# Far chunks of a chunked scan before a tanh network: log rows broadcast by DMA, y and state in one product, C B^T of two chunks at a time; the first chunks' state in its own bank

## The chip, the core and the metric

The kernel runs on one core of one Trainium2 chip. The metric is the device time of one execution in microseconds; the median of several runs is given. The core has five engines that run side by side: TensorE (PE), VectorE (DVE), ScalarE (ACT), GpSimd (POOL), and SyncE (SP), which here issues every DMA.

## The reference

Inputs: `x` (4, 8, 768, 32), decays `a` (4, 8, 768), `B` and `C` (4, 8, 768, 16), all float32; weights `w_in` (256, 2048) and `w_out` (2048, 256), float64.

```python
for c in range(nc):                       # chunks of 32 steps in the reference
    la = log_a[:, :, sl]
    cum = np.cumsum(la, axis=-1)
    L = np.exp(cum[:, :, :, None] - cum[:, :, None, :]) * causal
    M = np.einsum('bhin,bhjn->bhij', Cc, Bc) * L
    y_intra = np.einsum('bhij,bhjd->bhid', M, xc)
    y_inter = np.einsum('bhin,bhnd->bhid', Cc, state) * np.exp(cum)[:, :, :, None]
    y[:, :, sl] = y_intra + y_inter
    Bx = np.einsum('bhjn,bhjd->bhjnd', Bc, xc) * np.exp(cum[:, :, -1:] - cum)[:, :, :, None, None]
    state = np.exp(np.sum(la, axis=-1))[:, :, None, None] * state + np.sum(Bx, axis=2)
...
x = y.transpose(0, 2, 1, 3).reshape(3072, 256)
h = x @ w_in
g = h - np.tanh(h)
out = (g @ w_out).astype(np.float32)
```

## The kernel before

**The scan.** The result does not depend on the chunk length, so the kernel cuts each batch of 768 steps into seven chunks of 112 (`Q`), the last of 96; there are 28 chunks, 0 to 27. On the 128 partitions of a chunk's tiles the first 16 (`N`) hold the incoming state and the other 112 the steps, so state and steps go through the same products. For each chunk:

- `att`: PE makes C B^T of the eight heads (`bc` holds both; 32 rows a product, four products side by side). In `bc` POOL puts the 16x16 identity (`idn`) in the state's rows.
- `lt`: the decays between steps. For chunks 0 to 2 (`first_tile`) PE sums the logs into `cp` in a `ph` bank, and ACT takes the exponential with `ncum` as bias, one instruction for each head. For all later chunks (`chunk_a`) the log differences come as PE products in bfloat16 from three-part splits of the running sums: `lt_c` (ones and parts) times `rt_c` (parts and signs) into the first half of the `att` tile, and ACT takes one exponential over all heads. The parts go out to DRAM once (`cum3`, `put_parts`) and come back in small loads (`get_parts`), in two slices `SPAN`.
- DVE multiplies `att` into `lt`, POOL cuts it to the causal part (`affine_select`).
- `chunk_y`: PE multiplies `x` with `lt` into `y` (eight products of 112 columns), and `x` with the decayed `B` (`bw`, made by POOL in `prep`) into the next state in the same bank (eight products of 32 columns). ACT copies the state into the first 16 rows of the next chunk's `x` (four copies) and rounds `y` into `xh`; DVE makes the remainder `xl`.

**The network** runs transposed on token tiles (`WIDTH`: four of 256, four of 512). Each factor is a rounded part and a remainder (`wh`, `wl`, `xh`, `xl`, `gh`, `gl`), and three of the four part products are taken. `mm1` is the first product into a `ph` bank (two exist), `act` the tanh (ACT), the subtraction (DVE), rounding (ACT) and remainder (DVE), and `mm2` the second product into `po0`/`po1`. The weights arrive as float64 bits in `raw` and are turned into `wh` and `wl` by ACT and DVE (`conv`). The first four tiles run in sweeps over four blocks of the middle dimension (`SWEEPS`), so that work can begin while weights come in; the other four run over all 16 at once.

**Order.** All work goes through `Order`: each piece names its engine, a cost, what it reads and writes; a list planner (`search`) with these costs and priorities then fixes the order in which each engine's queue gets its instructions. Each engine runs its queue in order. Chunks from `JOINT` (10) on are called far here; in them C B^T of a chunk is issued together with y of the chunk before it as one PE step, and y takes a `ph` bank instead of `po1`.

## Time and profile before

| | |
|---|---|
| median of 3 runs | 338.89 us (338.74 to 338.98) |
| the profiled execution | 338.04 us, its span 336.3 us |
| busy: PE, DVE, ACT, POOL | 323.7, 227.8, 193.5, 51.4 us |
| DMA | 22.85 MB |

Columns of the profile's lines: in a timeline the start and the duration in us, the engine, the line of the kernel, the operation, what it writes and reads, and in brackets the idle time ahead with what ended it. A PE row's duration reaches past the start of the next row because products are pipelined, so steps of PE are measured from start to start. An f32 product shows as two records (x8 for four products). In a table of stretches: the stretch, its length, then for PE, PE's weight loads, DVE, ACT and POOL the busy time and instructions, then the granted PE clock (1.00 is full speed), the DMA share and GB/s. In a list of waits: who waited for whom, us in total, times, longest.

### The profile page before, as it was taken

What the parts mean: (1) busy time and instruction counts of PE and PEld (TensorE: products, weight loads), DVE (VectorE), ACT (ScalarE), POOL (GpSimd) and SP (SyncE); (2) the same over time, 40 slices, a digit from 0 to 9 for tenths busy, and PEclk for the clock granted to TensorE, in tenths of its full rate; (3) what the DMA queues carried; (4) which work ended last, traced back from release to release, by engine and by line L of the source; (5) the groups of instructions that cost most, each with busy time, mean ns of one, the idle gap of its engine ahead of it and who ended that gap; (6) DMA issues with size and microseconds to landing.
All of it is one profiled execution on the core that took longest, in us unless ns stands there. A gap on an engine that the chain in (4) does not pass through costs nothing.

```text
span 336.3 us, 6854 instructions
## 1 busy us (share of the span) xinstructions
PE 323.7 (96%) x2764; PEld 273.5 (81%) x2764; DVE 227.8 (68%) x335; ACT 193.5 (58%) x399; POOL 51.4 (15%) x69
## 2 busy tenths in 40 slices
PE   8666999999999999999999999999999999999995
PEld 7545889999999999877787777877787787888884
DVE  5979989999899866565655575555565554644452
ACT  8857589677476434555565564555455553544441
POOL 1546442120300111011112012111011010000000
PEclk9957799999999999999999999999999999999999
DMA  6567835441000015302111110300010000100001
GB/s 197 185 207 261 248 127 188 141 125 59 2 1 2 2 33 178 119 7 71 44 48 43 32 56 34 107 2 1 2 62 3 0 2 0 62 2 0 0 2 62
DMA packets 12111, 22.85 MB, mean 68 GB/s; under 512 B 2672, under 2 KB 5400, under 8 KB 12080
## 3 DMA queue, kind: packets, MB, share of 16 engines
q1 hardware_dynamic: 12080, 22.42, 20.7%
q8 instruction: 22, 0.36, 0.5%
q14 instruction: 9, 0.07, 0.1%
HBM read 19.10 MB, written 3.32 MB: 67 GB/s over the span
## 4 chain that ended last, share of the span: by engine, by line
PE 91%; ACT 3%; SPq 2%; DVE 1%; DMA 1%; issue 1%; POOL 1%; DVEq 0%; ACTq 0%
PE o L611 41%; PE ph L557 41%; PE y L495 4%; PE att L449 3%; PE att L444 2%; ACT lt L391 1%; SPq L790 1%; PE y L503 1%; SPq L793 1%; DVE lt L457 1%; POOL lt L460 1%; DMA a_sb<-a_d 1%; DMA rt_c<-cum 0%; ACT L719 0%; ACT wv L290 0%
## 5 line engine op out<-in xcount | busy, mean ns | idle before, releaser
L571 ACT ACTIVATE g<-ph 128x512 f32<-128x512 f32 x96 | 57.5, 599 | 70.0 <-PE ph L557 68.5
L575 DVE TENSOR_TENSOR g<-ph,g 128x512 f32<-128x512 f32 x96 | 65.9, 688 | 43.9 <-ACT g L571 43.8
L585 DVE TENSOR_TENSOR gl<-g,gh 128x512 fp32r<-128x512 f32 x96 | 68.5, 715 | 34.9 <-ACT gh L579 33.4
L557 PE MATMUL ph<-xh,wh 128*128 128x256 f32 (+1 forms) x256 | 84.9, 342 | 0.0
L557 PE MATMUL ph<-xh,wl 128*128 128x256 f32 (+1 forms) x256 | 83.6, 337 | 0.0
L579 ACT CAST gh<-g 128x512 fp32r<-128x512 f32 x96 | 59.5, 620 | 39.4 <-DVE g L575 35.4
L611 PE MATMUL o<-gh,wh 128*128 128x256 f32 (+1 forms) x256 | 72.6, 345 | 0.0
L611 PE MATMUL o<-gl,wh 128*128 128x256 f32 (+1 forms) x256 | 70.9, 338 | 0.0
L611 PE MATMUL o<-gh,wl 128*128 128x256 f32 (+1 forms) x256 | 70.8, 338 | 0.0
L557 PE MATMUL ph<-xl,wh 128*128 128x256 f32 (+1 forms) x256 | 65.6, 338 | 0.0
L460 POOL TENSOR_SCALAR_AFFINE_SELECT lt<-lt 128x896 f32<-128x896 f32 (+1 forms) x25 | 28.5, 1142 | 197.3 <-DVE lt L457 159.7
L557 PEld LDWEIGHTS ph<-xh,wh 128*128 128x128 f32 x256 | 48.6, 190 | 7.0 <-issue 1.3
L557 PEld LDWEIGHTS ph<-xh,wl 128*128 128x128 f32 x256 | 48.6, 190 | 5.2
L557 PEld LDWEIGHTS ph<-xl,wh 128*128 128x128 f32 x256 | 44.1, 190 | 5.3
L611 PEld LDWEIGHTS o<-gh,wh 128*128 128x128 f32 x256 | 41.8, 190 | 6.2 <-issue 0.3
L611 PEld LDWEIGHTS o<-gl,wh 128*128 128x128 f32 x256 | 41.8, 190 | 5.2
L611 PEld LDWEIGHTS o<-gh,wl 128*128 128x128 f32 x256 | 41.8, 190 | 4.9
L457 DVE TENSOR_TENSOR lt<-att,lt 128x896 f32<-128x896 f32 (+1 forms) x25 | 26.7, 1068 | 9.9 <-ACT lt L453 9.6
L453 ACT ACTIVATE lt<-att 128x896 f32<-128x896 f32 (+1 forms) x25 | 22.6, 905 | 4.9 <-PE att L449 4.6
L495 PE MATMUL y<-lt,x 128*32 128x112 f32 (+1 forms) x448 | 17.6, 278 | 5.8 <-POOL lt L401 3.4
L508 ACT COPY x<-y 16x64 f32<-16x64 f32 x96 | 19.5, 203 | 6.5 <-DVE xl L516 5.1
L495 PEld LDWEIGHTS y<-lt,x 128*32 128x32 f32 x448 | 10.5, 114 | 13.3 <-issue 6.0
(69 smaller groups left out, 221.9 us busy)
## 6 DMA issues: line engine op xcount, KB each, us to landing
raw<-w_d SPq DMA_DIRECT2D x16, 512.0 KB
...
rt_c<-cum SPq DMA_DIRECT2D x8, 4.6 KB
```

Of the source, the lines that this page charges most:

```text
L449: nc.tensor.matmul(out=at_[:, i, 2:4, :], lhsT=bb[r], rhs=cc[r, :, 0:q], start=True, stop=True)
L453: nc.scalar.activation(k["l"][:, :, 0:q].rearrange("p (i w) q -> p i w q", i=4), k["a"][:, :, 0:2, :], AF.Exp)
L457: nc.vector.tensor_tensor(out=lt, in0=k["a"][:, :, 2:4, :], in1=lt, op=ALU.mult)
L460: nc.gpsimd.affine_select(out=k["l"][:, :, 0:q], in_=k["l"][:, :, 0:q], pattern=[[0, H], [1, q]], compare_op=ALU.is_ge, fill=0.0, base=N, ...
L495: nc.tensor.matmul(out=y[D * h : D * h + D, hg * Q : hg * Q + q], lhsT=d["x"][:, cg, P * hg + D * h : P * hg + D * h + D], rhs=k["l"][:, 4 ...
L508: nc.scalar.copy(grp[(ck + 1) // CPG]["x"][0:N, (ck + 1) % CPG, 2 * D * i : 2 * D * i + 2 * D], k["y"][D * i : D * i + N, H * D : H * D + ...
L557: nc.tensor.matmul(out=ph[:, i * w : i * w + w], lhsT=w_[:, u, 0, k, j * P : (j + 1) * P], rhs=(xh, xl)[p][:, k, ts], start=p == 0 and k = ...
L571: nc.scalar.activation(g, gs[t, f][0], AF.Tanh)
L575: nc.vector.tensor_tensor(out=g, in0=ph, in1=g, op=ALU.subtract)
L579: nc.scalar.copy(gh, gs[t, f][1])
L585: nc.vector.tensor_tensor(out=gl, in0=g, in1=gh.bitcast(F32), op=ALU.subtract)
L611: nc.tensor.matmul(out=po[t, seg][e], lhsT=w_[:, u, 1, j, e * P : (e + 1) * P], rhs=g[:, i * w : i * w + w], start=f == seg[0] and k == 0 ...
```

## The change

Four parts, and the planner's numbers with them.

1. *Log rows by DMA.* For far chunks the running sums themselves (`rows`, float32) go to a DRAM tensor `cumr`, and for each far chunk one load broadcasts its eight rows of 128 to all partitions, straight into the `lt` tile (`chunk_l`, issued three chunks ahead; `NL` goes from 3 to 4). ACT takes the exponential in place with `ncum` as bias, one instruction for each head, and POOL cuts. The second slice of `lt_c`/`rt_c`, its ones (ACT), signs (DVE) and small loads (SP) are gone; the signs of the first slice are made by POOL ahead of its other work. The far `att` holds no logs.
2. *y and state in one product.* The `lt` tile of a far chunk is 128 wide: POOL writes the decayed `B` in the first 16 columns of each head (in place of `bw`), and the y product of 128 columns gives the state, transposed, in the first 16 columns. DVE transposes it (`fn_t`) into a tile `s`, from which ACT copies.
3. *C B^T of two chunks at a time* in the `att` tile, with every second far y.
4. *State of chunks 0 to 4 in its own bank* `po0` (`z`), as a step of its own that does not need `lt`.

The planner gets a priority bonus (`URGE`) on the first chunks' work, a rule that lets a piece wait shortly for a more urgent one (`LOOK`), and changed costs.

```diff
-NPH, NL, NSW, NRAW, NGB, LAG, WARM = 2, 3, 4, 2, 3, 2, 8
+NPH, NL, NSW, NRAW, NGB, LAG, WARM = 2, 4, 4, 2, 3, 2, 8
+APART, URGE = 5, 3.0
...
+            soon = [(prio[j], r, j) for r, j in wait[e] if r < t + self.LOOK * self.ops[i][1] and prio[j] + r - t < prio[i]]
...
-            prio = [-rstart[i] - self.ops[i][1] + self.JITTER * rng.uniform(-1, 1) for i in range(n)]
+            prio = [-rstart[i] - self.ops[i][1] - self.urge[i] + self.JITTER * rng.uniform(-1, 1) for i in range(n)]
...
-            if ck in (0, 2):
-                s = ck // 2
-                sl = SPAN[s]
+            if ck == 0:
                 for w in range(2):
-                    op("DVE", (0.3, 0.8)[s], lambda w=w, sl=sl: nc.vector.tensor_scalar(
-                           out=rt_c[:, w, sl], in0=lt_c[:, sl, N:P], scalar1=par[:, w : w + 1], scalar2=None, op0=ALU.mult),
-                       r=[l_c[s], "par", k["n_l"][1]], w=[r_c[s]])
+                    op("POOL", 0.95, lambda w=w: signs(w), r=["par"], w=["rt_c"])
...
+    def chunk_l(ck):
+        d, k, q, cg = grp[ck // CPG], chs[ck], qlen(ck), ck % CPG
+        n_l = k["n_l"] = [slot("lt", NL)]
+        def fn_d():
+            k["whole"] = p3.tile([P, H, P], F32, tag="lt", name=f"lt{ck}", bufs=NL)
+            k["l"] = k["whole"][:, :, N:P]
+            nc.sync.dma_start(out=k["whole"].rearrange("p h m -> p (h m)"),
+                              in_=cumr[ck].rearrange("h m -> (h m)").unsqueeze(0).broadcast_to([P, H * P]))
+        def fn_e():
+            for h in range(H):
+                nc.scalar.activation(k["l"][:, h, 0:q], k["l"][:, h, 0:q], AF.Exp, bias=ncum[:, h, ck : ck + 1])
+        def fn_b():
+            nc.gpsimd.tensor_tensor(out=k["whole"][:, :, 0:N], in0=d["braw"][:, cg].rearrange("p (h n) -> p h n", h=H),
+                                    in1=wdec[:, :, ck : ck + 1].broadcast_to([P, H, N]), op=ALU.mult)
+        op("SP", 0.42, fn_d, r=["cumr"], w=n_l, dma=4 * KB)
+        if ck % CPB != CPB - 1:
+            op("POOL", 0.6, fn_b, r=["wdec", "bi", d["n_b"]], w=n_l)
+        op("ACT", 2.2, fn_e, r=["ncum", "tab"], w=n_l)
+        op("POOL", 1.1, lambda: cut(ck), w=n_l)
...
+        def fn_p():
+            at_ = ps_a.tile([P, 4, 4 * P], F32, tag="att", name=f"att{ck}")
+            at_ = at_[:, :, 0 : 4 * Q].rearrange("p i (k q) -> p i k q", k=4)
+            for j in range(2):
+                bb, cc = operands(ck + 1 + j)
+                a_ = chs[ck + 1 + j]["a"] = at_[:, :, 2 * j : 2 * j + 2, 0 : qlen(ck + 1 + j)]
+                for i in range(4):
+                    r = slice(32 * i, 32 * i + 2 * N)
+                    nc.tensor.matmul(out=a_[:, i], lhsT=bb[r], rhs=cc[r, :, 0 : qlen(ck + 1 + j)], start=True, stop=True)
...
-                    nc.tensor.matmul(out=y[D * h : D * h + D, hg * Q : hg * Q + q],
+                    nc.tensor.matmul(out=y[r, hg * P : hg * P + P] if both else v[r, hg],
                                      lhsT=d["x"][:, cg, P * hg + D * h : P * hg + D * h + D],
-                                     rhs=k["l"][:, 4 * hg + h, 0:q], start=True, stop=True)
-            if not last:
+                                     rhs=k["whole"][:, 4 * hg + h] if both else k["l"][:, 4 * hg + h, 0:q],
+                                     start=True, stop=True)
+            if not last and not far and not apart:
+                fn_s()
...
+        def fn_t():
+            k["s"] = p2.tile([P, 2, D], F32, tag="s", name=f"s{ck}")
+            nc.vector.transpose(out=k["s"], in_=k["y"][:, 0 : 2 * P].rearrange("p (g m) -> p g m", g=2)[:, :, 0:D])
...
+        if apart:
+            n_z = slot("po0", 1)
+            op("PE", 0.3, fn_s, r=[d["p_x"][cg], d["n_bw"]], w=[n_z])
+            copies(n_z)
+        if JOINT - 1 <= ck < NCK - 1 and (ck + 1 - JOINT) % 2 == 0:
+            n_a = slot("att", 1)
+            op("PE", cost + 0.92, lambda: (fn_p(), fn()), r=r + [grp[(ck + 1) // CPG]["n_bc"]], w=w + [n_a])
+            for j in range(ck + 1, ck + 3):
+                op("DVE", 1.08, lambda j=j: fn_m(j), r=[n_a], w=chs[j]["n_l"])
...
-    op("ACT", 0.9, lambda: ones(0), w=[l_c[0]])
-    op("ACT", 2.2, lambda: ones(1), r=["tab"], w=[l_c[1]])
+    op("ACT", 0.9, ones, w=["lt_c"])
...
+    for i in range(2):
+        op("SP", 0.42, lambda i=i: put_rows(i), r=["rows"], w=["cumr"], dma=KB // 2)
```

PE's queue at chunk 15 of the far stage before: `ph` and `o` are the network's products, the number behind a name is the chunk or tile and step. The four products of logs come first, then C B^T of chunk 16, y of chunk 15, its state.

```order
L557 MATMUL ph4_4_2064<-xl_100,wh_80 128x512 x2
L444 LDWEIGHTS lt_c_102
L444 MATMUL att16_2071<-rt_c_103,lt_c_102 128x224
...
L449 MATMUL att16_2071<-bc8_1961 128x224 x4
L495 MATMUL y15_2080<-lt15_2020,x7_1882 32x112 x8
L503 MATMUL y15_2080<-x7_1882,bw7_1918 16x32 x8
L611 MATMUL o4_0_0_2037<-gh4_2_2047,wh_80 128x512
```

The same place now; the rows after the break are y of chunk 16, with no C B^T beside it.

```order
L629 MATMUL ph4_4_2050<-xl_100,wh_80 128x512 x2
L528 MATMUL att15_2061<-bc8_1981 128x224 x8
L541 MATMUL y15_2070<-lt15_1869,x7_1909 32x128 x8
L683 MATMUL o4_0_0_2009<-gh4_2_2033,wh_80 128x512
...
L683 MATMUL o4_0_1_2010<-gl4_5_2146,wh_80 128x512
L541 MATMUL y16_2170<-lt16_2037,x8_2093 32x128 x8
L629 MATMUL ph4_8_2183<-xh_99,wh_80 128x512
```

The products of a step were four of logs, four of C B^T, eight of y and eight of the state; now C B^T of chunks 16 and 17 stands with y15, y has 128 columns, and nothing else is left; y16 stands directly ahead of ph4_8, behind an o step.

ACT's queue behind y15 before. L571 is the tanh, L513 the rounding of y, L579 that of g, L508 the state's copies, L453 the exponential.

```order
L513 CAST xh_99<-y15_2080 128x2x112
L579 CAST gh4_4_2108<-g4_4_2098 128x512
L508 COPY x8_2050<-y15_2080 16x64 x4
L453 ACTIVATE lt16_2124<-att16_2071 128x896
L571 ACTIVATE g4_5_2134<-ph4_5_2112 128x512
```

ACT's queue behind y16 now, where L643 is the tanh, L569 the rounding of y, L651 that of g, L564 the state's copies and L494 the eight exponentials.

```order
L643 ACTIVATE g4_7_2164<-ph4_7_2148 128x512
L651 CAST gh4_6_2166<-g4_6_2155 128x512
L651 CAST gh4_7_2181<-g4_7_2164 128x512
L569 CAST xh_99<-y16_2170 128x2x112
L494 ACTIVATE lt17_2133<-lt17_2133,ncum_93 128x112 x8
L643 ACTIVATE g4_8_2219<-ph4_8_2183 128x512
L564 COPY x8_2093<-s16_2190 16x2x32 x4
```

One exponential of 896 columns, which waited for `att`, became eight of 112, which wait for the load; they stand between the rounding of y and the next tanh, and the state's copies behind that tanh.

PE's queue at the start before, from C B^T of chunk 1 (written to the tile `att0`) to y of chunk 2:

```order
L384 MATMUL att0_179<-bc1_138 128x224 x4
L374 MATMUL cp2_0_232<-upto_83,la_87 128x112 x4
L495 MATMUL y0_247<-lt0_172,x0_159 32x112 x8
L503 MATMUL y0_247<-x0_159,bw0_222 16x32 x8
L374 MATMUL cp2_1_271<-upto_83,la_87 128x112 x4
L495 MATMUL y1_311<-lt1_216,x0_159 32x112 x8
L503 MATMUL y1_311<-x0_159,bw0_222 16x32 x8
L444 LDWEIGHTS lt_c_102
...
L495 MATMUL y2_352<-lt2_276,x1_207 32x112 x8
L503 MATMUL y2_352<-x1_207,bw1_243 16x32 x8
```

And now, from C B^T of chunk 2:

```order
L397 MATMUL att0_178<-bc1_161 128x224 x4
L541 MATMUL y1_298<-lt1_214,x0_128 32x112 x8
L553 MATMUL z1_311<-x0_128,bw0_226 16x32 x8
L541 MATMUL y2_341<-lt2_274,x1_203 32x112 x8
...
L456 MATMUL att3_356<-bc1_161 128x224 x4
L629 MATMUL ph0_0_367<-xh_99,wh_80 128x256
...
L553 MATMUL z2_387<-x1_203,bw1_380 16x32 x8
```

The state products became `z` in their own tile; C B^T of chunk 3 stands behind y of chunk 2, and the first big product ahead of that chunk's state.

SP's queue at the start before (the small loads are the rows on `lt_c` and `rt_c`; `raw` are weights, `bc`, `x` and `braw` a chunk pair's inputs; `braw1` stood earlier):

```order
L784 DMA cum3_104<-parts_101 112x6x128
L252 DMA x1_207<-x_d 128x512
L240 DMA bc2_237<-bc_d 128x704
L790 DMA lt_c_102<-cum3_104 6x1x896 x2
L793 DMA rt_c_103<-cum3_104 3x7x112 x4
```

The same stretch of SP's queue now:

```order
L859 DMA cum3_105<-parts_101 112x6x128
L281 DMA raw1_188<-w_d 128x1024 x2
L262 DMA x1_203<-x_d 128x512
L865 DMA lt_c_102<-cum3_105 6x1x896
L868 DMA rt_c_103<-cum3_105 3x7x112 x2
...
L868 DMA rt_c_103<-cum3_105 3x7x112 x2
L271 DMA braw1_95<-bn_d 112x256
L250 DMA bc2_337<-bc_d 128x704
```

The second weights and `x1` now stand directly ahead of the small loads, and `braw1` and `bc2` behind them.

More of the change, by code (lines that the diff above doesn't have):

```diff
@@ L491, in fn, with fn_m @@
+        def fn_m(j):
+            l = chs[j]["l"][:, :, 0 : qlen(j)].rearrange("p (i w) q -> p i w q", i=4)
+            nc.vector.tensor_tensor(out=l, in0=chs[j]["a"], in1=l, op=ALU.mult)
         def fn():
[L492 removed]
+            y = k["y"] = (ps_h if far else ps_o).tile([P, BANK], F32, tag=tag, name=f"y{ck}")
+            v = k["yv"] = y[:, 0 : 2 * P].rearrange("p (g m) -> p g m", g=2)[:, :, N : N + q]
+            both = far and not last
@@ L725, in stay, with ones, signs @@
                                   in_=idn[0:N].unsqueeze(1).broadcast_to([N, CPG * H, N]))
-    def ones(i):
-        v = lt_c[:, SPAN[i]].rearrange("p c m -> p (c m)")
+    def ones():
+        v = lt_c.rearrange("p c m -> p (c m)")
         nc.scalar.copy(v, nc.const_aps.tensor(1.0, (P, 1), F32).broadcast_to(v.shape))
+    def signs(w):
+        v = rt_c[:, w].rearrange("p c q -> p (c q)")
+        nc.gpsimd.tensor_scalar(out=v, in0=nc.const_aps.tensor(1.0, (P, 1), F32).broadcast_to(v.shape),
+                                scalar1=par[:, w : w + 1], scalar2=None, op0=ALU.mult)
     def warm():
```

139 lines of the change are left out of this document (77 added, 62 removed).

## Prediction

> **What bounds the kernel now.** I read the page first: span, TensorE's (PE's) share, and the engines' shares of the chain that ended last.
>
> ```profile
> span 336.3 us, 6854 instructions
> PE 323.7 (96%) x2764; PEld 273.5 (81%) x2764; DVE 227.8 (68%) x335; ACT 193.5 (58%) x399; POOL 51.4 (15%) x69
> PE 91%; ACT 3%; SPq 2%; DVE 1%; DMA 1%; issue 1%; POOL 1%; DVEq 0%; ACTq 0%
> ```
>
> PE is busy for 96% of the span and is 91% of the chain, so what counts is PE's own work and the places where PE waits or runs slowly. Next come PE's waits, complete, and then the table of stretches (PE busy stands first after the length, the granted clock after the five engines).
>
> ```profile
> PE y L495 <- POOL lt L401: 3.4, 1, 3.4
> PE y L495 <- POOL bw L338: 1.6, 1, 1.6
> PE att L444 <- DVE lt L457: 1.1, 1, 1.1
> PE y L495 <- POOL lt L460: 0.8, 1, 0.8
> PE warm L736 <- PEq L896: 0.8, 1, 0.8
> PE att L444 <- DVE lt L396: 0.6, 1, 0.6
> PE att L444 <- DMA rt_c<-cum: 0.3, 1, 0.3
> ...
> 18.00:28.00 10.00, 7.96 (x107) 6.17 (x103) 7.87 (x13) 6.06 (x15) 4.21 (x5) 0.50 0.83 278
> 28.00:32.00 4.00, 2.23 (x80) 1.83 (x76) 3.97 (x5) 3.17 (x11) 2.57 (x4) 0.93 0.64 233
> 32.00:38.50 6.50, 5.66 (x65) 4.36 (x61) 6.47 (x9) 4.25 (x11) 3.87 (x3) 0.51 0.73 215
> 38.50:140.00 101.50, 101.50 (x1101) 96.63 (x1098) 88.14 (x121) 64.01 (x121) 15.98 (x16) 1.00 0.27 86
> ```
>
> The waits sum to 8.6 us, each happens once, and none lies on the big products. Leaving out 0.8 of the warm-up, 7.8 us are PE waiting for the first seven chunks. From 38.5 us on PE is busy without a gap at full clock; before that it also loses to the clock: half of 7.96, 7% of 2.23 and half of 5.66, together 4.0 + 0.2 + 2.8 = 7.0 us. So there are two places to gain: the first 38.5 us, and the PE time of the chunks once PE is full.
>
> **Far chunks (10 to 27): PE time.** These rows of PE's timeline are one joint far step (C B^T of chunk 16 and y of chunk 15), one joint step whose y is a batch's last chunk (96 columns, no state), and the last y alone. Columns: start, duration, line, product.
>
> ```profile
> 157.54 0.62 PE L557 MATMUL ph<-xl,wh 128*128 128x512 f32 x2
> 158.09 0.28 PE L444 MATMUL att<-rt_c,lt_c 9*128 9x224 bf16 x4
> 158.20 0.57 PE L449 MATMUL att<-bc 32*128 32x224 f32 x8
> 158.69 0.59 PE L495 MATMUL y<-lt,x 128*32 128x112 f32 x16
> 159.10 0.30 PE L503 MATMUL y<-x,bw 128*16 128x32 f32 x16
> 159.33 0.50 PE L611 MATMUL o<-gh,wh 128*128 128x512 f32 x1
> 159.67 0.40 PE L611 MATMUL o<-gh,wl 128*128 128x512 f32 x1
> ...
> 199.58 0.28 PE L444 MATMUL att<-rt_c,lt_c 9*128 9x224 bf16 x4
> 200.19 0.54 PE L495 MATMUL y<-lt,x 128*32 128x96 f32 x16
> 200.65 0.50 PE L611 MATMUL o<-gh,wh 128*128 128x512 f32 x1
> ...
> 278.19 0.54 PE L495 MATMUL y<-lt,x 128*32 128x96 f32 x16
> 278.66 0.51 PE L611 MATMUL o<-gh,wh 128*128 128x512 f32 x1
> ```
>
> I go by differences of starts. The step takes 159.33 - 158.09 = 1.24 us: logs 0.11, C B^T 0.49, y 0.41, state 0.23. Of the y alone (0.47) and the y behind a C B^T (200.65 - 200.19 = 0.46) I learn that 0.46 for 96 columns includes the drain that the state product hides in the full step. Reaching the next product costs 0.34 (159.67 - 159.33) where the others take 0.23, so leaving a step costs 0.11.
>
> *y and state in one product.* Before, y of 112 columns and state take 0.41 + 0.23 = 0.64. A product's time grows with its columns. If all of the 0.46 did, 128 columns would take 0.61; with a fixed drain of 0.15 in it (0.46 less the 0.31 that grows) they take 0.31 x 128/96 + 0.15 = 0.56. The rows of leaving and entering show that there is a drain, so I take 0.57, a gain of 0.07. Fifteen of the 18 far chunks have a state: 1.0 us. Ends: 0, and 0.23 less the 0.06 of wider columns, 15 x 0.17 = 2.6.
>
> *C B^T of two chunks at a time, no log products.* Before, a chunk pays 0.11 + 0.49 = 0.60, a pair 1.20. After, a pair pays two groups of the 0.49 kind back to back. The trace has no two such groups in a row. From above they cost an isolated group of the start (in the last table: 7.69 - 7.09 = 0.60) and one of 0.49, 1.09. From below I take the drain into the next shape, about the 0.11 of above, off one of them: 0.49 + 0.38, about 0.86. The joint rows are nearer than the isolated one, so I take 0.95. Nine pairs gain 9 x 0.25 = 2.2 us; ends 9 x 0.11 = 1.0 and 9 x 0.34 = 3.1. Each chunk still interrupts the big products once, for its y, so entering and leaving are paid as often as before.
>
> Far sum: 3.2 us, ends 1.0 and 5.7.
>
> **What the far chunks add beside PE.** The price of the exponential rises from one instruction of 905 ns to eight of 128x112; at the start eight such took 2.06. The first row below is the group of the old one; the next two are the work that frees a `ph` bank after the product that ended near 158.0.
>
> ```profile
> L453 ACT ACTIVATE lt<-att 128x896 f32<-128x896 f32 (+1 forms) x25 | 22.6, 905 | 4.9 <-PE att L449 4.6
> ...
> 158.25 0.60 ACT L571 ACTIVATE g<-ph 128x512 f32<-128x512 f32 x1 [0.77 <-PE ph L557]
> ...
> 158.89 0.69 DVE L575 TENSOR_TENSOR g<-ph,g 128x512 f32<-128x512 f32 x1 [0.68 <-ACT g L571]
> ```
>
> ACT gets 18 x 1.15 = 21 us more on 193.5, far from PE's 324. Off PE's path this costs nothing as long as no bank comes late. A bank is read out 1.6 us after its product (158.89 + 0.69 = 159.58, less 158.0). With two `ph` banks, y takes one: y16 stands behind one o step (1.37, six products of 0.23) and ph4_8 directly behind y16, so ph4_7's bank must be free 1.37 + 0.10 + 0.57 = 2.0 us after it: 0.4 to spare. Then the burst (2.06) runs ahead of ph4_8's tanh. That tanh starts 0.4 + 2.06 = 2.5 us after y16 ends instead of 1.7; its bank is asked for again after ph4_8, o, ph4_9, o, 5.5 us after y16, and is free by 2.5 + 1.3 = 3.8 to 3.9. Hidden, with 1.6 us as cover. DVE gets 15 transposes of 64 columns, each below the 0.69 of the 512-column row; POOL a state product of 128 columns in place of 256. The row loads are 18 x 512 KB; at the 278 GB/s of the second table one takes 1.9 us, and they are issued three chunks ahead. I cost all of this at nothing. If ACT's cover goes, PE waits for a `ph` bank (first rival).
>
> **The start.** ACT, DVE and SP rows that the change removes or moves, then PE's marks: an isolated C B^T, y of chunk 2, and the point from which PE is full.
>
> ```profile
> 5.52 2.09 ACT L729 CAST lt_c<-const-float32-1.0 128x2304 bf16<-128x2304 f32 x1
> 7.52 2.06 ACT L391 ACTIVATE lt<-cp,ncum 128x112 f32<-128x112 f32 x8
> ...
> 11.52 1.14 DVE L422 TENSOR_SCALAR rt_c<-lt_c,par 128x784 bf16<-128x784 bf16 x2
> 20.06 1.41 DVE L422 TENSOR_SCALAR rt_c<-lt_c,par 128x2016 bf16<-128x2016 bf16 x2
> ...
> 12.73 1.61 SPq L790 DMA_DIRECT2D lt_c<-cum  x2
> ...
> 5.23 1.93 PE L374 MATMUL cp<-upto,la 128*128 128x112 f32 x16
> 7.09 0.66 PE L384 MATMUL att<-bc 32*128 32x224 f32 x8
> 7.69 0.65 PE L770 MATMUL pq<-la,after 128*128 128x224 f32 x2
> 21.22 0.97 PE L495 MATMUL y<-lt,x 128*32 128x112 f32 x16
> 38.49 0.38 PE L557 MATMUL ph<-xh,wh 128*128 128x256 f32 x1
> ```
>
> The chain there alternates ACT (exponential), DVE (product), POOL (cut), PE (y). (1) ACT's second fill of ones goes. The first exponentials then wait only for the running sums; PE makes chunk 0's in two halves from 5.23 to 7.09, so the first half is there near 6.3 and ACT starts then instead of at 7.52: 1.2 us. (2) DVE's signs for the first slice (1.14, directly ahead of chunk 1's product) go to POOL before its first work; (3) those of the second slice (1.41, ahead of chunk 3's product) go away: DVE is busy 7.87 of 10 us in the stretch from 18. Together 1.2 + 1.1 + 1.4 = 3.7 us off one chain. (4) The state of chunks 0 to 4 has its own bank: the state products no longer wait for the cut; as steps of their own they enter and leave PE's array once more, mostly while PE has time: -0.2 us. (5) SP: the small loads stood behind the signs (their first start, 12.73, is just behind DVE's 11.52 + 1.14 = 12.66). Now they can go earlier, but x of chunk 2 and the second weights stand before them in SP's queue and `braw1` and `bc2` behind them, so I count no gain; the twelve tiny loads of the second slice disappear while SP has time. So 3.5 us, ends 0 (a new wait behind what SP now brings later) and 7.8 (all PE waits but the warm-up). Nearest to the rows are the removed pieces themselves, hence 3.5.
>
> Between 38 and 60 us the order puts C B^T and y of several near chunks side by side; two interruptions fewer, at 0.10 + 0.11 each, are 0.4 us.
>
> **Sum.** 3.2 + 3.5 + 0.4 = 7.1 us. The profiled execution took 338.04 (1.74 around its span), which becomes 330.9; the median of the runs is 338.89, 0.85 above that execution, so I forecast 331.8 us.
>
> **Rivals.**
> - *ACT bursts stop PE* (slower). The place is the tanh behind each burst, with 1.6 us of cover. It costs PE time from a burst of 2.06 + 1.6 = 3.7 us on, and outweighs the 7.1 us when PE loses 0.4 us at each of 18 chunks, from 4.1 us a burst. Were each of the eight as long as the tanh of 512 columns (0.60), a burst would be 4.8 us and PE would lose 18 x 1.1 = 20 us: 352. Against it: eight took 2.06 at the start.
> - *The start gives nothing.* POOL's signs hold back its first copy, or `braw1`, `bc2` or x of chunk 2 land late, and PE is full no sooner: 338.9 - 3.6 = 335.3. For it: SP's order. By a rule of the Trainium skill (Perfetto Trace Analysis, Optimizing Scalar/DVE Operations) VectorE and GpSimd share an SBUF read port, so moving work from one to the other might not help; by that rule the sum is this rival's. No row here shows POOL's signs; they run at 2 to 5 us, where DVE does little.
> - *The clock stays up.* If the waits become short enough, half of the 7.0 us lost to the clock returns too: 331.8 - 3.5 = 328.3. Against it: the row from 18 to 28 shows 0.50 with PE busy 80% of it. By the Trainium skill (TensorE: Matmul & The Clock Gate, What's actually happening) about 3.4 us of sustained work open the gate and an idle window as long shuts it; the row shows that 80% is not yet sustained, and whether the new start is, no row says.
> - *The joined products cost what they did* (wide y 0.64, pair 1.20): 338.9 - 3.9 = 335.0.
>
> **Chances.** The forecast 0.52; start gives nothing 0.20; clock stays up 0.20; joined products no cheaper 0.03; bursts 0.05. The range of 327.5 to 336.0 takes in both large rivals with the far sum's lower end (335.3 + 0.7) and some of its upper; outside remain the bursts and parts of the clock's case and of the far upper end, under 0.2. About 0.2% (0.7 us) is what a measurement of this kernel can tell from no change: faster 0.93, within 0.02 (start lost and the far end low), slower 0.05.
>
> **What would show it.** In the profile after: a y of 128x128 with about 0.57 to the next start and no L503 rows in the far stage; a pair of C B^T at 0.86 to 1.09; PE's waits before 40 us under 5 us and none on `ph`; ACT near 212 us busy; the first unbroken big product at 34 to 36 us instead of 38.49. I am wrong if PE waits for DVE or ACT beyond 60 us, if the row loads appear as releasers, or if the first y's come no sooner.

## Result and profile after

| kernel | median of its runs, us | ratio to before, 95% interval |
|---|---|---|
| before | 339.02 (336.31 to 340.14) | 1 |
| after | 336.70 (335.20 to 339.57) | 0.9947 [0.9924, 0.9970] |
| after, 448 unused bytes ahead of some buffers | 334.27 (333.31 to 335.85) | 0.9878 [0.9842, 0.9914] |

The change gains 2.3 us where I forecast 7.1; 336.70 lies 0.7 us above my range. Both kernels spread over some 4 us from run to run, mostly with the granted clock, which differs between executions in the start (its mean over a run of after is 0.995 in the fastest, 335.20 us, and 0.978 in one of 338.40). The third row is the changed kernel with the one mend that the experiments led to; no later version that keeps all work is measurably faster. The profiled execution of after took 337.02 us. From its page, the lines that answer to those of before:

```profile
span 335.1 us, 6403 instructions
PE 321.2 (96%) x2452; PEld 269.7 (80%) x2452; DVE 226.3 (68%) x346; ACT 218.3 (65%) x524; POOL 57.0 (17%) x77
PE 82%; DMA 8%; DVE 4%; ACT 2%; SPq 1%; issue 1%; POOL 0%; POOLq 0%
```

PE's share of the chain fell from 91% to 82%; the 8% of DMA are loads of weights, `braw` and `bc` in the first 52 us, on which more below. PE's waits, and the table of stretches of after:

```profile
PE y L541 <- ACT wh L321: 3.1, 1, 3.1
PE att L451 <- DVE lt L464: 2.0, 3, 1.1
PE y L541 <- DVE xl L572: 1.5, 1, 1.5
PE y L541 <- issue: 1.3, 1, 1.3
...
PE ph L629 <- DVE xl L572: 0.2, 1, 0.2
```

```profile
18.00:28.00 10.00, 8.25 (x90) 6.49 (x91) 9.42 (x13) 6.54 (x18) 5.11 (x5) 0.52 0.78 252
28.00:32.00 4.00, 3.03 (x67) 2.37 (x67) 2.99 (x6) 2.79 (x7) 2.13 (x3) 0.91 1.03 366
32.00:38.50 6.50, 5.31 (x82) 4.64 (x82) 6.47 (x8) 5.18 (x15) 2.94 (x4) 1.00 0.82 232
38.50:62.00 23.50, 20.45 (x289) 18.09 (x287) 23.38 (x30) 20.05 (x45) 11.23 (x9) 1.00 0.67 228
```

The last stretch is new. Before, PE was busy for all of these 23.5 us and DVE for 21.6:

```profile
38.50:62.00 23.50, 23.50 (x324) 21.15 (x324) 21.60 (x29) 19.61 (x41) 7.91 (x7) 1.00 0.48 156
```

Now DVE is busy for 23.38 of 23.5, and PE stands for 3 us. The row with `issue` is the wait of y10: there the profile names no releaser. The far steps of after on PE:

```profile
147.58 1.04 PE L528 MATMUL att<-bc 32*128 32x224 f32 x16
148.55 0.65 PE L541 MATMUL y<-lt,x 128*32 128x128 f32 x16
149.12 0.50 PE L683 MATMUL o<-gh,wh 128*128 128x512 f32 x1
...
159.04 0.64 PE L541 MATMUL y<-lt,x 128*32 128x128 f32 x16
159.62 0.50 PE L629 MATMUL ph<-xh,wh 128*128 128x512 f32 x1
```

The pair of C B^T costs 148.55 - 147.58 = 0.97 (I took 0.95), the wide y 0.57 and 0.58 (0.57).

**Where the time went.** I compare the start of one y in both kernels, at equal work on PE before it. y6 starts at 40.05 before and at 41.23 after, but after has three half-steps (ph or o of one tile and slice, 1.41 us for 256 columns) more behind it: a lead of 40.05 - 41.23 + 4.23 = 3.05. y10 and y27 have the same work ahead in both.

| lead over before, us | y6 | y10 | y27 | difference of spans |
|---|---|---|---|---|
| after | 3.05 | 61.62 - 61.39 = 0.23 | 278.19 - 276.39 = 1.80 | 336.3 - 335.1 = 1.2 |

So the start brought 3.05, the near stage (y6 to y10) lost 2.8, the far chunks brought 1.6 instead of 3.0 (my 3.2 less the first pair, which stands ahead of y10), and PE's last 54 us, in which both kernels do the same work, lost 0.6 more.

These are single executions. That of before lies 0.98 us under its median and that of after 0.32 over its own, so the spans differ by 1.2 us where the medians differ by 2.3. The near stage is steadier: from y6 to y10 the changed kernel takes 61.39 - 41.23 = 20.16 us, and 20.0 to 20.2 in the seven other profiles of this order in which the stage's work is whole. Before takes 21.57 with three half-steps more, so 17.34 at equal work.

### The profile page after: what moved, and what is told of

The parts are those of the page before. It is cut to its first block, busy times and chain, and to the rows that moved or that the text cites. A ratio compares the mean times of both kernels' runs of the same rounds, so it can differ in the third digit from the quotient of the medians.

```text
span 335.1 us, 6403 instructions
## 1 busy us (share of the span) xinstructions
PE 321.2 (96%) x2452; PEld 269.7 (80%) x2452; DVE 226.3 (68%) x346; ACT 218.3 (65%) x524; POOL 57.0 (17%) x77
## 4 chain that ended last, share of the span: by engine, by line
PE 82%; DMA 8%; DVE 4%; ACT 2%; SPq 1%; issue 1%; POOL 0%; POOLq 0%
PE o L683 39%; PE ph L629 38%; DMA raw<-w_d 5%; PE y L541 3%; PE att L528 2%; DMA bc<-bc_d 2%; DMA braw<-bn_d 1%; ACT wv L300 1%; ACT lt L404 1%; DVE gl L657 1%; ACT x L566 0%; SPq L871 0%; DVE g L647 0%; DVE wm L305 0%; DVE xl L572 0%
## 5 line engine op out<-in xcount | busy, mean ns | idle before, releaser
L643 ACT ACTIVATE g<-ph 128x512 f32<-128x512 f32 x96 | 57.2, 597 | 67.6 <-PE ph L629 65.9
L629 PE MATMUL ph<-xh,wh 128*128 128x256 f32 (+1 forms) x256 | 85.8, 346 | 0.0
L629 PE MATMUL ph<-xh,wl 128*128 128x256 f32 (+1 forms) x256 | 84.6, 341 | 0.0
L657 DVE TENSOR_TENSOR gl<-g,gh 128x512 fp32r<-128x512 f32 x96 | 68.8, 716 | 20.0 <-ACT gh L651 18.9
L651 ACT CAST gh<-g 128x512 fp32r<-128x512 f32 x96 | 59.5, 620 | 26.4 <-DVE g L647 25.4
L494 ACT ACTIVATE lt<-lt,ncum 128x112 f32<-128x112 f32 (+1 forms) x144 | 41.9, 377 | 0.0
L541 PE MATMUL y<-lt,x 128*32 128x128 f32 (+2 forms) x448 | 18.0, 275 | 6.4 <-ACT wh L321 3.1
L532 DVE TENSOR_TENSOR lt<-att,lt 128x896 f32<-128x896 f32 (+1 forms) x18 | 19.0, 1058 | 0.0
L564 ACT COPY x<-s 16x64 f32<-16x64 f32 x60 | 14.4, 241 | 1.4 <-DVE s L559 0.7
```

The source lines that it names most:

```text
L494: nc.scalar.activation(k["l"][:, h, 0:q], k["l"][:, h, 0:q], AF.Exp, bias=ncum[:, h, ck : ck + 1])
L532: nc.vector.tensor_tensor(out=l, in0=chs[j]["a"], in1=l, op=ALU.mult)
L541: nc.tensor.matmul(out=y[r, hg * P : hg * P + P] if both else v[r, hg], lhsT=d["x"][:, cg, P * hg + D * h : P * hg + D * h + D], rhs=k["wh ...
L564: nc.scalar.copy(to.rearrange("p (g h d) -> p g h d", g=2, h=4)[:, :, i], k["s"][D * i : D * i + N])
L629: nc.tensor.matmul(out=ph[:, i * w : i * w + w], lhsT=w_[:, u, 0, k, j * P : (j + 1) * P], rhs=(xh, xl)[p][:, k, ts], start=p == 0 and k = ...
L643: nc.scalar.activation(g, gs[t, f][0], AF.Tanh)
```

## The loss in the far stage: 64 bytes of address

Two half-steps ph and two half-steps o of 512 columns take this long where nothing else is on PE (starts of the same product, before and then after, from PE's timelines):

```profile
300.77 0.39 PE L611 MATMUL o<-gh,wh 128*128 128x512 f32 x1
...
306.26 0.39 PE L611 MATMUL o<-gh,wh 128*128 128x512 f32 x1
```

```profile
301.94 0.40 PE L683 MATMUL o<-gh,wh 128*128 128x512 f32 x1
...
307.50 0.40 PE L683 MATMUL o<-gh,wh 128*128 128x512 f32 x1
```

5.49 before, 5.56 after. By half-steps behind 280 us, as means of 12 to 14 each: before o 1.373 and ph 1.373; after o 1.396 and ph 1.382 (the expectations below have 1.399 and 1.379, with the same sum). The excess lies in the o half-steps and in what follows them: a ph behind an o takes 1.382, the two that stand behind a ph take 1.374. The first two runs asked whether this is chance, the next two tried what else I suspected (GpSimd's cuts, ACT's bursts).

**e1_before, e1_after**: both kernels again.

> The kernel before, profiled again. In the first profile a product of 512 columns took 0.2287 us from start to start, in the changed kernel's 0.2325, 1.5% more, also after 280 us where both do the same work; that is 128 half-steps x 6 x 0.0038 = 2.9 us. Theory P1 (a trait of the execution, not of the change): the pitch here moves by 1% or more between executions, so this profile can show 0.232 too. Theory P2 (a trait of the changed kernel): 0.2287 here again, within 0.0005.

> The changed kernel, profiled again. P1: its 512-column pitch differs from 0.2325 by more than 0.001. P2: 0.2325 again. Theory S (the lead won at the start is given back between 42 and 62 us because y of chunks 7 and 10 wait for late ACT, DVE and POOL work): the waits of 1.5 us at y7 and 1.3 us at y10 come again at the same instructions. Rival: they are chance and do not come again. Time about 0.995 of before.

Measured: 338.44 (1.0003 [0.9971, 1.0035]) and 336.36 (0.9950 [0.9922, 0.9979]); o 1.373 and 1.396. The pitch, the time from one product to the next, is a trait of the changed kernel, and so are the two waits of the near stage, 1.33 at y7 and 1.26 at y10 here.

**e1_small_cut, e1_short_exp**: in after, same order, the cuts of chunks 3 to 9 on 16 columns of one head; one of the eight exponentials of each far chunk.

```
-        nc.gpsimd.affine_select(out=k["l"][:, :, 0:q], in_=k["l"][:, :, 0:q], pattern=[[0, H], [1, q]],
+        h, q = (H, q) if ck >= JOINT else (1, 16)
+        nc.gpsimd.affine_select(out=k["l"][:, 0:h, 0:q], in_=k["l"][:, 0:h, 0:q], pattern=[[0, h], [1, q]],
...
-            for h in range(H):
+            for h in range(1):
```

> Left out: the causal cut of chunks 3 to 9, which becomes a POOL instruction of 16 columns of one head; order and everything else as in the changed kernel. Theory S1 (POOL's cuts stretch DVE's two-input instructions in SBUF, gl 0.68 to 1.4-1.7 us, and this makes y7 late): gl of 1.4 us becomes 0.7 before 50 us, y7's wait of 1.5 falls under 0.5, the waits on DVE before 40 us shrink, 1.5 to 3 us faster than the changed kernel. Theory S2 (y7 is late because the planner put y6 and y7 side by side on one bank): y7 still waits about 0.9 us (rounding and remainder of y6), under 1 us faster.

> Left out: seven of the eight far exponentials of each chunk (one head only); order and everything else as in the changed kernel. Theory B1 (the bursts of eight, 2.35 us with their neighbours, are what makes y10 late and cost PE here and there later): y10's wait of 1.3 us goes, 1.3 to 3 us faster than the changed kernel. Theory B2 (y10 is late through DVE, which has weight conversion ahead of chunk 10's product): y10 still waits about 1 us, under 0.7 us faster, and PE's rows after 65 us are unchanged.

Measured: 335.99 (0.9930 [0.9898, 0.9963]) and 336.88 (0.9955 [0.9924, 0.9985]). Neither changes the pitch (o 1.397 and 1.395). Without the bursts nothing is gained: from y10 to y27 after takes 276.39 - 61.39 = 215.00 us and the kernel with short bursts 275.97 - 60.93 = 215.04. The bursts, which I feared, are not what costs in the far stage. At y7 the small cuts leave 0.88 of the 1.49, at y10 they leave 1.56; the short bursts change neither.

The addresses that the two programs give their buffers pointed on: wh, wl, xh and xl lie where they did, while the three buffers each of g, gh and gl (2048 bytes a partition) begin 8640 bytes lower, since `lt_c` and `rt_c` have become smaller and `lt` larger. Before, they begin 448 bytes behind a multiple of 512; after, at a multiple of 512.

**e2_pad, e3_pad448, e3_g448, e3_before_64**: unused bytes, the same order of instructions.

```
     rt_c = cp.tile([P, 2, NEAR.stop - NEAR.start, Q], BF16, name="rt_c")
+    pad = cp.tile([P, 2160], F32, name="pad")        # e2_pad: 8640 bytes
+    pad = cp.tile([P, 112], F32, name="pad")         # e3_pad448: 448 bytes
...
+            if t == f == 0:                              # e3_g448: directly ahead of g
+                p3.tile([P, 112], F32, tag="pad", name="pad", bufs=1)
             g = p3.tile([P, BANK], F32, tag="g", name=f"g{t}_{f}")
...
     rt_c = cp.tile([P, 2, NCK, Q], BF16, name="rt_c")    # the kernel before
+    pad = cp.tile([P, 16], F32, name="pad")          # e3_before_64: 64 bytes
```

> The changed kernel with one unused tile of 8640 bytes a partition between rt_c and the buffers that follow, in the same order: g, gh, gl, the weight buffers and the rest stand at the addresses again that they have in the kernel before. In the changed kernel an o step of six 128x512 products takes 1.399 us and a ph step 1.379 late in the run, before 1.373 both. Theory P-address (the place of the buffers sets it): both are back at 1.373 to 1.376 after 280 us, and the kernel is 2.0 us faster than the changed one (64 o steps by 0.026 and 64 ph steps by 0.006), near 334.5 us. Theory P-program (the stream of instructions or the history of the run sets it): 1.399 and 1.379 again, 336.4.

> The changed kernel, same order, with an unused tile of 448 bytes instead of 8640 behind rt_c. The buffers of 2048 bytes (g, gh, gl) then begin at another distance than the ones of before, but 448 bytes behind a multiple of 512, as there; in the changed kernel they begin at multiples of 512. Theory R (the remainder of the address sets the pitch): an o step is back at 1.373, and the time near 334.3, as with 8640 bytes. Theory L (the region does, or the distance to the weights): 1.399 stays, 336.4.

> The 448 bytes stand directly ahead of g, so that only g, gh and gl move, while lt, the weight buffers, x and bc stay where the changed kernel has them. If the place of g, gh and gl is what counts (an o step reads gh and gl as its moving operand): 1.373 as with the 448 bytes behind rt_c. If it is another buffer's place: 1.399.

> The kernel before, same order, with an unused tile of 64 bytes behind rt_c: g, gh and gl then begin at multiples of 512, as in the changed kernel, and nothing else is changed. Theory R: o steps at 1.399 and ph steps at 1.379 to 1.388 late in the run, and the time 2.0 us longer, near 340.9. Theory L: 1.373, and the time of before, 338.9.

| run | g begins, modulo 512 | o half-step | us | ratio |
|---|---|---|---|---|
| e2_pad | 448 | 1.373 | 334.29 | 0.9871 [0.9841, 0.9902] |
| e3_pad448 | 448 | 1.373 | 334.19 | 0.9845 [0.9822, 0.9868] |
| e3_g448 | 448 | 1.373 | 335.90, one run | none |
| e3_before_64 | 0 | 1.396 | 340.44 | 1.0035 [1.0015, 1.0055] |

The same two rows, of e2_pad and of e3_before_64:

```profile
302.29 0.39 PE L683 MATMUL o<-gh,wh 128*128 128x512 f32 x1
...
307.79 0.39 PE L683 MATMUL o<-gh,wh 128*128 128x512 f32 x1
```

```profile
302.80 0.40 PE L611 MATMUL o<-gh,wh 128*128 128x512 f32 x1
...
308.36 0.40 PE L611 MATMUL o<-gh,wh 128*128 128x512 f32 x1
```

5.50 and 5.56: 64 unused bytes give the kernel before the slow pitch, 448 take it from the changed one, in both regions tried, and moving g, gh and gl alone is enough. The single run of e3_g448 lost its time in the start (y6 at 42.26); from y10 to y27 it takes 213.56 us, as e3_pad448 does, where after takes 215.00. The remainder is worth 2.1 to 2.5 us of the changed kernel. In the kernel before it costs 1.2 by the medians, with an interval from 0.5 to 1.9, less than the 2.0 expected; in the profiles it costs 1.6 between y10 and y27 alone (218.18 against 216.57).

With the pad y27 leads by 278.19 - 274.23 = 3.96 in e2_pad. From y10 to y27 the lead grows by 3.0 in e3_pad448, e3_g448 and e5_pad448: the far term of my sum was right. In e2_pad it grows by 3.6; the 0.6 more lies between y10 and y11, and why stays open.

A rival is that the slow products meet accesses of ACT, DVE or a DMA. Near the end of after everything but PE stands still, and the products are slow all the same. The stretch (PE, weight loads, DVE, ACT, POOL, clock, DMA), then nine products of after, the first 0.25 us ahead of the stretch, and nine of before at the same place of its run, where the others stand still from 329.90 on:

```profile
328.60:330.60 2.00, 2.00 (x10) 1.65 (x9) 0.00 (x0) 0.00 (x0) 0.00 (x0) 1.00 0.00 0
```

```profile
328.35 0.39 PE L683 MATMUL o<-gh,wh 128*128 128x512 f32 x1
...
330.44 0.40 PE L683 MATMUL o<-gh,wh 128*128 128x512 f32 x1
```

```profile
329.61 0.39 PE L611 MATMUL o<-gh,wh 128*128 128x512 f32 x1
...
331.67 0.39 PE L611 MATMUL o<-gh,wh 128*128 128x512 f32 x1
```

2.09 us after, 2.06 before. So the other engines aren't needed for it. What is left beside the products is PE's own weight loads (1.65 of the 2.00 us); whether these two reads meet isn't shown.

## The loss in the near stage: VectorE

y7 waits 1.49 us for y6's remainder, whose bank it takes; y10 waits 1.26 for a `ph` bank. What stands ahead of both on DVE, POOL and ACT in after:

```profile
41.97 1.47 DVE L657 TENSOR_TENSOR gl<-g,gh 128x512 fp32r<-128x512 f32 x1
43.37 0.34 DVE L572 TENSOR_TENSOR xl<-y,xh 128x192 fp32r<-128x192 f32 x1
...
46.55 0.38 DVE L572 TENSOR_TENSOR xl<-y,xh 128x224 fp32r<-128x224 f32 x1
46.85 1.70 DVE L317 SCALAR_TENSOR_TENSOR wv<-wv,wm 128x1024 uint32<-128x1024 uint32 x1
...
57.80 1.89 DVE L317 SCALAR_TENSOR_TENSOR wv<-wv,wm 128x1024 uint32<-128x1024 uint32 x1
59.61 1.08 DVE L532 TENSOR_TENSOR lt<-att,lt 128x896 f32<-128x896 f32 x1
60.61 1.27 DVE L647 TENSOR_TENSOR g<-ph,g 128x512 f32<-128x512 f32 x2
```

```profile
41.52 1.38 POOL L476 TENSOR_SCALAR_AFFINE_SELECT lt<-lt 128x896 f32<-128x896 f32 x1 [1.90 <-DVE lt L464]
42.87 1.07 POOL L350 TENSOR_TENSOR bw<-braw,wdec 128x256 f32<-128x256 f32 x1
45.57 1.90 POOL L476 TENSOR_SCALAR_AFFINE_SELECT lt<-lt 128x896 f32<-128x896 f32 x1 [1.62 <-DVE lt L464]
...
57.62 0.99 POOL L476 TENSOR_SCALAR_AFFINE_SELECT lt<-lt 128x896 f32<-128x896 f32 x1 [5.10 <-ACT lt L494]
58.58 1.38 POOL L497 TENSOR_TENSOR lt<-braw,wdec 128x128 f32<-128x128 f32 x1
```

```profile
55.20 2.35 ACT L494 ACTIVATE lt<-lt,ncum 128x112 f32<-128x112 f32 x8
57.57 0.60 ACT L643 ACTIVATE g<-ph 128x512 f32<-128x512 f32 x1
```

y6's remainder (43.37) stands behind a gl that took 1.47 instead of 0.68, and y10's bank is freed by the first g of 60.61, behind a conversion (57.80) and chunk 10's product (this is read from the order: the first g, 0.68 long, ends at 61.29 and y10 starts at 61.39). The product in turn could not come earlier than the burst of 55.20 and its cut (57.62): two causes of the same wait, one covering the other. The long instructions have both inputs in SBUF, and POOL runs beside them; 46.55, which reads PSUM, keeps its 0.38 beside the cut of 45.57. With the small cuts the same gl took 0.68 to 0.69.

**e2_light_conv, e4_ablate3**: in after's order, four of DVE's five instructions of conversions 2 to 4 on 64 of 1024 columns; then these, the small cuts, one exponential of eight in chunks 10 and 11, and the 448 bytes together.

```
+        few = slice(0, 32) if 2 <= u <= 4 else slice(0, 512)
...
-            nc.vector.scalar_tensor_tensor(out=wm[u][:, s], in0=wv[u][:, s], scalar=3, in1=wm[u][:, s],
+            nc.vector.scalar_tensor_tensor(out=wm[u][:, s, few], in0=wv[u][:, s, few], scalar=3, in1=wm[u][:, s, few],
```

> The changed kernel, same order, with four of VectorE's five instructions of the weight conversions 2, 3 and 4 on 64 of 1024 columns (weights 2 to 4 are then not those of the reference): some 10 us less work on VectorE between 30 and 60 us, 2.4 of them directly ahead of chunk 10's product. Theory D (VectorE is the bound of the near stage, 38 to 62 us): PE's waits at y7 (1.5) and y10 (1.3) fall below 0.3 each and the kernel gains 2.5 to 3.5 us, near 333.5. Theory N (the near stage is bound by what comes over SP and by ACT): other waits take their place, and less than 1 us is gained, 335.5 or more.

> The changed kernel with the 448 bytes, same order, with three pieces taken away together: VectorE's part of conversions 2 to 4 on 64 of 1024 columns, GpSimd's cuts of chunks 3 to 9 on 16 columns of one head, one of eight exponentials in chunks 10 and 11 (part of the output is then not the reference's). Alone, each left a wait: conversions 0.9 and 0.6 at y7 and y10, cuts 0.9 and 1.6, exponentials 1.5 and 1.3. Theory T (each wait has two covers, one behind the other): both waits fall below 0.3, the lead over the kernel before is carried from y6 to y10, and the time is 331.3 to 332.3. Theory N (something else holds these two products): a wait of over 0.6 stays at one of them.

Measured: 334.58 (0.9881 [0.9851, 0.9911]) and 333.08 (329.94 to 334.60; 0.9836 [0.9788, 0.9883]). Waits of the first, then of the second:

```profile
PE y L543 <- DVE xl L574: 0.9, 1, 0.9
...
PE y L543 <- issue: 0.6, 1, 0.6
```

```profile
PE y L544 <- DVE wv L312: 0.9, 1, 0.9
```

y10 waits 1.26 with everything, 0.59 without the conversions, nothing without all three pieces: theory T holds there, and the burst with its cut is the likely second cause, though the two weren't taken away apart from each other. At y7 0.9 stays in both runs, against theories D and T: y6 and y7 follow each other through one bank (read from the wait for y6's remainder, not tested).

| from y6 to y10, us | |
|---|---|
| before, less three half-steps | 17.34 |
| after | 20.16 |
| e1_small_cut | 58.52 - 39.18 = 19.34 |
| e2_light_conv | 59.55 - 41.21 = 18.34 |
| e4_ablate3 | 57.37 - 39.73 = 17.64 |

Of the 2.8 us lost, 1.8 come back without the conversions and 2.5 without all three. All loads of the stage are still there in these runs, so the loads that the page puts on the chain do not hold it. The medians show less of it: e2_light_conv gains 1.8 to 2.1 on after, but e4_ablate3 only 1.1 to 1.2 on the padded kernel, with 1.6 us open to either side, and 333.08 lies above the 331.3 to 332.3 of theory T.

**e3_defer, e4_moved, e5_moved2**: all work kept, with the pad, conversions 3 and 4 held back by an added dependence (planned anew), then nine and ten steps moved by hand in the finished order.

```
+            late = [misc["prod", {3: 8, 4: 10}[u]]] if u in (3, 4) else []         # e3_defer
...
+        for what, behind in self.moves:                                           # e4_moved, e5_moved2
+            queue.remove(what)
+            queue.insert(queue.index(behind) + 1, what)
...
+    op.moves = [(d["gl", 1, 0], d["xl", 6]), (d["burst", 10], d["row", 10]), (d["cut", 10], d["cut", 9]),
+                (d["wv", 4], d["xh", 9]), (d["prod", 10], d["xl", 9]), (d["lo", 3], d["gl", 2, 2]), (d["c2", 4], d["lo", 3]),
+                (d["c3", 4], d["xl", 10]), (d["c4", 4], d["g", 0, 4]), (d["hi", 4], d["tanh", 0, 6])]   # e5_moved2
```

> The changed kernel with the pad of 8640 bytes, and with VectorE's part of weight conversion 3 held back until the product of chunk 8, and that of conversion 4 until the product of chunk 10 (weights 4 are first used 18 half-steps behind y10). In the padded kernel y7 waits 1.5 us and y10 1.3. Theory Q (they wait behind conversions that the order put ahead of them on VectorE): both waits fall below 0.3 and the time to 332 to 333 us. Theory W (VectorE has no room anywhere in the near stage, so the work held back only delays others): waits of the same sum come elsewhere, and the time stays within 0.7 of 334.3.

> The changed kernel with the 448 bytes (334.2 us), all work kept and PE's order untouched; nine steps are moved by hand on the other engines: y6's remainder ahead of gl of the step before on VectorE; chunk 10's eight exponentials, its cut and its product as early as its logs are there; of weight conversion 4 ACT's part behind y9's copies, VectorE's first two behind gl of tile 2, its third behind the subtractions that free the ph banks of tile 3. Theory Q2 (y7 and y10 wait behind work that could stand elsewhere): y7's wait falls from 1.5 to about 0.6, y10's from 1.26 to below 0.2, no new wait over 0.3 comes, and the time is 1.5 to 2.2 us shorter, 332.0 to 332.7. Theory W (there is no room; the work moved makes other waits): within 0.5 of 334.2.

> As e4_moved, with its two faults mended: VectorE's and ACT's last parts of weight conversion 4 stand behind the first work of the second sweep (they are needed some 15 half-steps later), and the last part of conversion 3 stands behind y9's remainder and chunk 10's product. All work is kept. Theory Q2: y7 waits 0.6, y10 and the product that read pt's bank below 0.3, y9's remainder keeps PE below 0.3; by the 1.5 + 0.3 us that this leaves out of e4_moved (335.75, span 334.2) the time is near 333.5, and in any case below the padded kernel of the same call. Theory W: another wait of over 1 us comes, and the padded kernel stays ahead.

> The changed kernel with the 448 bytes again, on the same chip as e5_moved2: 334.2 us, y7 and y10 waiting 1.5 and 1.3. Its stretch from 18 to 28 us shows whether the granted clock of 0.83 in the profile of e3_pad448 belongs to the kernel (again near 0.8) or to the execution (0.50 to 0.55, as in the other profiles of this order).

Measured: 336.24 (0.9897 [0.9861, 0.9932]), 335.75 (0.9927 [0.9895, 0.9958]), 333.76 (0.9886 [0.9845, 0.9926]), and the padded kernel beside the last 334.27 (0.9878 [0.9842, 0.9914]): no order beats it measurably. e3_defer made y10's wait 2.16. The waits of e4_moved and of e5_moved2 that came in place of y10's:

```profile
PE o L687 <- ACT pt L709: 1.5, 1, 1.5
```

```profile
PE ph L633 <- DVE g L651: 1.2, 1, 1.2
```

y7 fell to 0.6 and y10's wait went, as planned, but the conversion put back came due later: 1.5 us behind ACT's part of it at 64.4, 1.25 behind DVE at 70.0. In e5_moved2 y10 comes 0.8 us earlier than in e5_pad448 (60.80 and 61.61), and y27 at the same time (275.14 and 275.17). In these three orders, work moved on the full engine returned as another wait (theory W); only work taken away helped.

## The start, and what belongs to the pairing

**e2_ones_back, e4_start_back**: in after's order, ACT's fill put back; then the fill and DVE's four instructions on signs, into scratch tiles that nobody reads.

```
+        if i:
+            nc.scalar.copy(more, nc.const_aps.tensor(1.0, (P, 1), F32).broadcast_to(more.shape))
...
+            if (ck, i) == (1, 0):
+                signs_back(7)
...
+            if ck == 3:
+                signs_back(18)
```

> The changed kernel, same order, with ACT's fill of 2304 columns put back ahead of the first exponentials, into a tile that nobody reads (4608 bytes, which move the buffers behind it by as much). Theory S (term 1 of the start stands and is carried to the end): y of chunk 2 comes 1.2 us later than 19.28 and the end is 1.2 us later, near 337.6. Theory F (VectorE's queue is the floor that chunk 10 waits for, and it does not start earlier with PE): y of chunk 2 is 1.2 later, but the waits at y7 and y10 shrink by as much, and the end is within 0.3 of the changed kernel, 336.4. The pitch of the o steps tells by the way whether a shift of another size matters: P-address leaves any value open, P-program says 1.399.

> The changed kernel in the same order, with what it took out of the start put back at its place: ACT's fill of 2304 columns ahead of the first exponentials, VectorE's two instructions of 784 columns ahead of chunk 1's first product and two of 2016 ahead of chunk 3's. Scratch tiles of 8640 bytes, so that g, gh and gl stand as in the padded kernel (334.2). My prediction's terms 1 to 3 (1.2 + 1.1 + 1.4 = 3.7 us on one chain) say 337.5 to 338. Theory H (ACT's fill costs half of its term, as the run with it alone suggests, and VectorE has idle time at both places): 335 to 336.

Measured: 336.97 (0.9954 [0.9928, 0.9981]) and 337.58 (0.9976 [0.9953, 0.9999]; buffers as in the padded kernel). Against 334.2 to 334.3 the removed pieces are worth 3.3 us, carried to the end (my terms 1 to 3: 3.7); its y10 stands 2.9 us behind that of e2_pad (64.11 and 61.26) and y27 3.4 (277.67 and 274.23). From y6 (43.92) to y10 it takes 20.19 us, and y7 and y10 wait 1.51 and 1.27: a start 2.9 us later leaves the near stage as it is. The fill alone moved y2 from 19.28 to 20.17, and the end by 0.3 to 0.6 with intervals of 1 us either way: whether its 1.2 is carried whole stays open. y2 of after, and of e4_start_back with its next wait:

```profile
19.28 0.97 PE L541 MATMUL y<-lt,x 128*32 128x112 f32 x16 [3.07 <-ACT wh L321]
```

```profile
20.41 0.97 PE L549 MATMUL y<-lt,x 128*32 128x112 f32 x16 [3.55 <-DVE xl L580]
27.88 0.38 PE L457 MATMUL att<-rt_c,lt_c 9*128 9x224 bf16 x4 [1.74 <-DVE lt L472]
```

**e2_old_start**: the far part with the start of before (`APART, URGE = 0, 0.0`, `LOOK = 0.0`, signs on DVE, both fills, twelve more small loads), planned anew.

> The far part alone: the changed kernel with the start of before (state of chunks 0 to 4 in y's bank, no urgency for the first chunks, signs by VectorE ahead of chunk 1's and chunk 3's products, both fills of ones on ACT, the twelve small loads; the signs and loads of the second slice go to a tile that nobody reads). Its two extra tiles have 8640 bytes together, so that the buffers stand where they do before. If the terms add up: y2 near 21.2 us, far stage with 3.6 us less PE time than before. Theory A (gains add; the near stage lost 2.8 us because of the new order and the pitch 2.0 by addresses): no waits on PE beyond 40 us and the pitch 1.373, so about 338.9 - 3.6 = 335.3, faster than the changed kernel. Theory B (the start is worth its 3.1 us at the end, and the pitch belongs to the far part's program): slower than the changed kernel, 338.5 or more.

Measured: 339.90 (1.0036 [1.0012, 1.0061]): theory A has the pitch right (o 1.373) and the time wrong. The order that the planner made has waits that neither kernel has:

```profile
PE y L544 <- DVE xl L575: 5.1, 2, 3.0
PE att L454 <- DMA rt_c<-cum: 3.5, 3, 1.3
```

It is 3.97 us behind before at y10 (65.59) and 1.11 at y27 (279.30): the far part brings 2.9 here too, but the start alone cannot be had this way, since the order is another.

**e4_no_pair**: C B^T of one chunk ahead of each y, with the pad.

```
-            for j in range(2):
+            for j in range(1):
...
-        if JOINT - 1 <= ck < NCK - 1 and (ck + 1 - JOINT) % 2 == 0:
+        if JOINT - 1 <= ck < NCK - 1:
```

> The changed kernel with the 448 bytes, with C B^T of one chunk ahead of each y instead of two ahead of each second y (all else of the far part kept; the order is planned anew, so that the near stage may differ). My prediction gave the pairing and the lost log products 0.25 a pair together. By the trace a pair costs 0.97 where two groups behind log products cost 0.98 and two log products 0.22. Theory J (the saving is the log products, the pairing itself is worth nothing): from y10 to y27 the lead over the kernel before grows as in the padded one (3.0 to 3.6 us), within 0.5. Theory K (a lone group is paid with entering, 0.60): it grows by 9 x 0.2 = 1.8 less.

Measured: 337.67 (0.9971 [0.9942, 0.9999]); from y10 (62.34) to y27 (277.64) the lead grows by 1.27 instead of 3.0. Theory K: a lone group costs 0.59 at each y,

```profile
158.30 0.66 PE L528 MATMUL att<-bc 32*128 32x224 f32 x8
158.89 0.64 PE L541 MATMUL y<-lt,x 128*32 128x128 f32 x16
```

two of them 1.18 where a pair costs 0.97. Pairing is worth 0.21 a pair, most of the 0.25 that I gave the whole step, and the eight pairs behind y10 make up the 1.7 that is missing; by the same rows, dropping the log products alone would have brought 0.02.

## Why the prediction was wrong

- *Far chunks, 3.2 us: right*, and in its parts (0.97 for 0.95, 0.575 for 0.57; 3.0 with the pad). The 0.31 in my reckoning of the wide y stands in no row; 0.41 x 96/112 = 0.35 is what the rows give, and with it the sum is 0.58.
- *The start, 3.5 us: right in size.* y2 at 19.28 (my pieces: 18.9), a lead of 3.05 at y6, 3.3 when put back. The first term was 0.9 and not 1.2: ACT's first exponential starts at 6.65 instead of 7.52. POOL's signs took 4.56 us for two, and DVE's three copies of `braw` beside them 1.36 instead of 0.69 (0.69 again in e2_old_start, where DVE makes the signs); PE's first running sums start at 5.57 instead of 5.23. This much of my second rival came true. PE's waits before 40 us sum to 6.1, where I expected under 5.
- *The step that failed first: "y of several near chunks side by side; two interruptions fewer are 0.4 us".* I counted PE's interruptions and did not ask whether DVE could follow. The row of before, shown above, had it: DVE busy for 21.60 of 23.50 us. The new order has five weight conversions on DVE ahead of chunk 10's product where the old one has four, and y7 close behind y6 in one bank. PE waits 1.49 us at y7, 0.23 at a `ph` product and 1.26 at y10, and the stage lost 2.8 us in place of the 0.4 that I gave it. The earlier start is not the cause: in e4_start_back the stage is as long. The wait at y10, as read above, is the condition that I named for being wrong (PE waits for DVE beyond 60 us).
- *The second: the cost of the pitch, which I took as unchanged.* It is 2.0 us over 64 half-steps o and 64 ph, by a shift of buffers that the change makes without saying it.
- *Bursts:* 2.35 us each where I took 2.06; ACT 218 where I wrote 212. They stop PE nowhere in the far stage; only at y10 do they count, as the likely second cause. My first rival was rightly rated low.
- *Clock:* from 32 to 38.5 us it is 1.00 instead of 0.51, from 18 to 28 still 0.52. Neither is fixed: the other profiles of the two kernels show 0.74 (e1_before) and 0.76 (e1_after) from 32 to 38.5. In the padded kernel the stretch from 18 to 28 differs between executions:

```profile
18.00:28.00 10.00, 8.05 (x112) 6.26 (x112) 9.80 (x14) 6.91 (x19) 5.34 (x6) 0.83 0.79 255
```

```profile
18.00:28.00 10.00, 8.27 (x91) 6.50 (x92) 9.43 (x13) 6.53 (x18) 5.41 (x5) 0.55 0.79 248
```

These are e3_pad448 and e5_pad448, one program. Their y6 start at 39.53 and 41.42, and the spans are 331.4 and 333.3: the 1.9 us are carried to the end. So that rival's gain is real and a matter of chance. The Trainium skill (TensorE: Matmul & The Clock Gate, What's actually happening) says that the gate watches a window that runs freely of the kernel's start, which fits; no run here shows the window.

Of the 4.8 us between the gain forecast and the gain measured the near stage accounts for 3.2 (-2.8 where I wrote 0.4) and the pitch for 2.1 to 2.5. That is 0.5 to 0.9 more than is missing, and the start fell short by 0.2 to 0.5 besides; the interval of the medians leaves 0.8 us open to either side.
